# Values loaded head by head, two weight loads moved up the queue and wider filler matmuls in a fused attention and feed-forward kernel

## The chip, the core and the metric

The kernel runs on one core of a Trainium2 chip. The time is device microseconds from launch to end. Three runs of the kernel before gave 101.67, 102.06 and 102.32 us; the median is 102.06 us. One further execution was profiled: it took 102.56 us, of which 100.8 us are its span, from the first to the last instruction. The remaining 1.76 us lie around the span.

Engine names follow the profile: PE is the matrix engine (PEld its weight loads), DVE, ACT and POOL are the vector, scalar and general engines, SP issues nearly all DMAs from one queue. Each engine works through its own instructions in program order.

## What is computed

Linear attention with a polynomial sketch, and behind it a gated feed-forward layer. Batch 4, heads 4, sequence 1088, head width 32, sketch width 8; model width 128, inner width 1536.

```python
def phi(x):
    a = np.einsum('rd,bhsd->bhsr', S1, x)
    b = np.einsum('rd,bhsd->bhsr', S2, x)
    return np.einsum('bhsi,bhsj->bhsij', a, b).reshape(*x.shape[:-1], r * r)
q_p, k_p = phi(q), phi(k)
kv  = np.einsum('bhsf,bhsd->bhfd', k_p, v)
z   = np.sum(k_p, axis=2)
num = np.einsum('bhsf,bhfd->bhsd', q_p, kv)
den = np.einsum('bhsf,bhf->bhs', q_p, z)[..., None] + 1e-06
attn = num / den                              # then heads side by side: x, 4352 x 128
out = (np.maximum(x @ w_gate, 0) * (x @ w_val)) @ w_out
```

## The kernel before

**Layout.** Partition `32*h + p` of `k_sb[b]` and `q_sb[b]` holds 34 consecutive tokens of head `h`. The values lie otherwise: partition `32*a + p` of `v32[b]` holds nine tokens (seven for `a` = 3) of each of the four heads, 1152 bytes a head, since there the tokens are the rows of a matmul. `load_v(eng, b, a)` (L212) fills 32 partitions with all heads; four calls, in the order 0, 2, 1, 3, fill one batch.

**Loads.** SP issues, in this order: keys and queries of batch 0, its four value loads (L236), then `load_w(0)`, `load_w(1)` (gate and value weights, a third at a time, 256 KB each: wg0, wv0, wg1, wv1), `load_wo(0)`, keys of batch 1, `load_w(2)` (wg2, wv2), two more thirds of the output weights, queries of batch 1 (L263 to L270). The weights land in the buffers that later hold keys, queries and values of other batches, and are then cast to 16 bits by ACT (L425) or POOL (L427); `CAST` (L418) says by which.

**The plan.** All other work is a list of operations, each with an engine, an assumed duration, its predecessors and a due time. `Plan.run` (L89) places them once, when the program is built: it picks the next operation by earliest start and due time, gives out PSUM banks, and the program is then recorded in the order of the planned starts (L1091 to L1100). So the constants of the plan (`LAND`, the assumed landing times; `T0`, `U`, the due times of the feed-forward units; `act`, `pool` and others, assumed durations) fix the order on every engine, but not when anything really runs. On the chip an operation waits for its semaphores, and what stands behind it on its engine waits with it.

**Names used below.** `vc b h`: ACT casts two heads of the values of batch b to 16 bits (`K.vc`, L598). `kv b`: PE multiplies key features with these values (L601); `kve` evacuates them. `qsk`, `qt2`, `bw`, `dn`, `rd`, `an`, `qphi`: sketch, transpose, denominator and features of a group of query tokens. `qtr` with `qpt` (PE and ACT), or `qtd` (a DMA transpose issued by SP, L867): the features transposed. `num`, `x`: attention output of the group, the input of the feed-forward layer. The layer is cut into 103 units: `g u` and `v u` on PE (L950, L962), `relu u` on ACT (L955), the product `h u` on DVE (L972), or, in every sixth unit, a copy on ACT (L967) and the product on POOL (L977), and `o u` on PE (L984). Groups of units end with a copy `oe` and a store `st`. Units 0 to 5, 6 to 11 and 12 to 23 belong to the token groups of batch 0, unit 24 is the first of batch 1.

**Fillers.** `warm(n)` (L326) records matmuls of zeros over `n` columns, 128 at a time, wherever the plan leaves PE idle ahead of the first unit.

Two of the five feature products of batch 0's keys are on DVE (`own`, L488). The change leaves that as it is.

Of the kernel before, what the change touches and what calls it, by code (L numbers as in the profile page):

```python
# [146 lines left out]
def kernel(  # L147
# [12 lines left out]
    nc = tc.nc  # L160
# [7 lines left out]
    NC = S // 32  # L168
# [40 lines left out]
    def load_k(eng, b):  # L209
        eng.dma_start(out=k_sb[b][:, 0:NC * D], in_=flat(k, b))  # L210

    def load_v(eng, b, a):  # L212
        w = KX * D
        n = w if a < 3 or b < B - 1 else (KX - 2) * D
        src = v[b, 0]
        eng.dma_start(
            out=v32[b][32 * a:32 * a + 32, :, 0:n],
            in_=bass.AP(src.tensor, src.offset + a * w, [[NC * D, 32], [S * D, H], [1, n]]))

    def wcols(w, lo, hi):  # L220
        return w[:, lo * 128:hi * 128]
# [11 lines left out]
    nc.sync.dma_start(out=k_sb[0][:, KH:NC * D], in_=flat(k, 0)[:, KH:])  # L233
    nc.sync.dma_start(out=q_sb[0][:, 0:QA], in_=flat(q, 0)[:, 0:QA])
    nc.sync.dma_start(out=q_sb[0][:, QA:], in_=flat(q, 0)[:, QA:])
    for a in (0, 2, 1, 3):  # L236
        load_v(nc.sync, 0, a)
    bz = [sb([128, 2, 128], FP16, f"bz{b}") for b in range(B)]
    zero = sb([128, 128], FP16, "zero")
    nc.vector.memset(zero, 0.0)  # L240
# [22 lines left out]
    load_w(0)  # L263
    load_w(1)
    load_wo(0)
    load_k(nc.sync, 1)
    load_w(2)
    load_wo(1)
    load_wo(2)
    nc.sync.dma_start(out=q_sb[1], in_=flat(q, 1))  # L270
# [2 lines left out]
        eng.dma_start(out=q_sb[b], in_=flat(q, b))  # L273

    def load_vs(b):
        for a in (0, 2, 1, 3):
            load_v(nc.sync, b, a)


    id16 = sb([2 * R, 2 * R], FP32, "id16")  # L280
# [25 lines left out]
    nc.vector.memset(bz[0], 0.0)  # L306
    for i in range(2):
        nc.vector.memset(kT[i][:, NC * 32:], 0.0)
    nc.vector.memset(v32[B - 1][96:128, :, (KX - 2) * D:], 0.0)
# [16 lines left out]
    def warm(n):  # L326

        while n >= 32:
            m = min(n // 32 * 32, 128)
            nc.tensor.matmul(PS[:, W_BANK, 0:m], zero, zero[:, 0:m], start=True, stop=True)  # L330
            n -= m

    warm(3584)
    S_BANK = 6
# [46 lines left out]
    P.banks[W_BANK] = 13.0  # L381
    P.banks[S_BANK] = 6.0
    l_sx = Lease()
    T0, U, SLACK = 11.0, 0.68, 0.25
    D1 = 0.2

    TURN = ["ACT"] * 3 + ["DMA"] * 7
# [8 lines left out]
        return cols / 960.0 + 0.085  # L396

    def act(cols):
        return cols / 1200.0 + 0.045

    def pool(cols):
        return cols * 0.00188 + 0.07

    LAND = {"k0a": 3.6, "S": 4.3, "k0b": 4.25, "q0a": 5.6, "q0b": 7.35, "v0": 9.95,
            "wg0": 10.35, "wv0": 11.0, "wg1": 11.65, "wv1": 12.3, "wo0": 12.95, "k1": 15.6,
            "wg2": 16.25, "wv2": 16.9, "wo1": 17.5, "wo2": 18.1, "q1": 19.5}
    land = {n: P.landed(n, t) for n, t in LAND.items()}
    P.free["DMA"] = LAND["q1"]

    def bank(l, i=0):  # L410
# [4 lines left out]
    sa_op = P.add("DVE", "SA", 0.22, make_SA, [land["S"]], rec=0.07)  # L415
    wb_op = P.add("DVE", "WB", 0.15, make_WB, [land["S"]], rec=0.07)

    CAST = {"wg0": "ACT", "wv0": "POOL", "wg1": "ACT", "wv1": "POOL", "wo0": "POOL",  # L418
            "wg2": "ACT", "wv2": "ACT", "wo1": "ACT", "wo2": "POOL"}
    wcast = {}  # L420

    def cast(w, i, eng):
# [9 lines left out]
                         rec={"ACT": 0.13, "DVE": 0.07, "POOL": 0.0}[e])  # L432


    def load(name, fn, after):
        n = 4 if name[0] == "v" else 1
        i = P.add("SP", f"{name} issue", 0.44 * n, fn, after, rec=1.95 - 0.44 * n)
        land[name] = P.add("DMA", name, 2.7 if n == 4 else 1.4, None, [i], rec=0.15)
# [5 lines left out]
    load("k3", lambda: load_k(nc.sync, 3), [wcast["wg0"], wcast["wv0"], land["q2"]])  # L444
    load("q3", lambda: load_q(nc.sync, 3), [wcast["wg1"], wcast["wv1"], land["q2"]])
    load("v3", lambda: load_vs(3), [land["v2"]])

    class K:


        def __init__(self, b, prev):
# [39 lines left out]
            for n, (lo, hi) in enumerate(cut):  # L491
# [11 lines left out]
                else:  # L503
                    phis.append(P.add("POOL", f"kphi {b} {lo}", pool(cols),
                                      lambda lo=lo, hi=hi: self.phi(nc.gpsimd, lo, hi), dep))
            vc = [P.add("ACT", f"vc {b} {h}", 0.58, lambda h=h: self.vc(h), [land[f"v{b}"]],
                        rec=0.13) for h in range(2)]
            lm = Lease()
            self.lm = lm
            self.kvs = []  # L510
# [120 lines left out]
    class Q:  # L631
# [3 lines left out]
        def __init__(self, b, x0, n, i, ks, qt1, old):  # L635
            self.b, self.x0, self.n, self.ks = b, x0, n, ks
            i = i % NS
            self.abc, self.an = q_abc[i], q_an[i]
            self.dn, self.rd, self.bw = q_dn[i], q_rd[i], bw[i]
            first = b == 0 and x0 == 0  # L640
            self.first = first
            name = f"{b},{x0}"
            cols = n * 32
            wcs = [kk.wc_op for kk in ks]
            if first:
                la, lc = Lease(), Lease()
# [13 lines left out]
                e, eng = "DVE", nc.vector  # L660

            else:
                self.l4 = [Lease(2), Lease(2)]
                s1 = P.add("PE", f"qsk {name}", cols / 600.0 + 0.28 + 0.37 * (n > NX),
                           self.sk, qt1 + wcs + [wq_op], take=self.l4)
# [25 lines left out]
            self.t2_op = t2  # L691
            self.last = []
# [106 lines left out]
    class G:  # L799


        def __init__(self, qs, b, ks, x0, n, i, col, old, how):
# [6 lines left out]
            if qs.first:  # L809
                for x in range(n):  # L810
                    phis.append(P.add("DVE", f"qphi {name} {x}", 0.31,
                                      lambda x=x: self.phi(nc.vector, x, x + 1), [qs.o4],
                                      drop=[qs.la], rec=0.07))
                qs.la.left -= n
            else:
                phis.append(P.add("POOL", f"qphi {name}", pool(n * 256),
                                  lambda: self.phi(nc.gpsimd, 0, n), [qs.o4] + old))
            if how == "DMA":
                pt = P.add("SP", f"qtd {name}", 1.28, self.xpose, phis + old, rec=0.7)
                pt = P.add("DMA", f"qtd {name}", 0.6, None, [pt], rec=0.5)  # L820
            else:
                lt = Lease()
# [84 lines left out]
    class F:  # L907


        def __init__(self, u, grp, qg, js, prev, old):  # L910
# [14 lines left out]
            vv = P.add("PE", f"v {u}", cost, self.v, [qg.x_op, wcast[f"wv{third}"]], take=[lv], due=t + 0.2)  # L925
            if self.pool:
                a2 = P.add("ACT", f"vcp {u}", act(cols), self.vcp, [vv], drop=[lv], rec=0.13,
                           due=t + 0.6)
                h = P.add("POOL", f"hp {u}", 1.18, self.hp, [a, a2, old], due=t + 1.3)
# [113 lines left out]
    for n, (b, x0, w, parts) in enumerate(sets):  # L1043
# [6 lines left out]
        for gb, y, m in parts:  # L1050
# [80 lines left out]
```

## Time and profile before

| what | value |
|---|---|
| median of three runs | 102.06 us |
| profiled execution | 102.56 us, span 100.8 us |
| PE busy | 95.1 us, 94% of the span |
| DVE, ACT, POOL busy | 83.8, 82.2, 59.9 us |
| feed-forward matmuls g, v, o on the chain that ended last | 18%, 17%, 19% of the span |
| fillers on that chain | 7% |
| granted PE clock | full in all 40 slices |
| DMA | 13.28 MB, mean 132 GB/s; the first 20 us carry over 270 GB/s in most slices |

The profile counts an engine as busy while one of its instructions runs, fillers included. The chain of waits goes back from the last instruction: at each step to what released it, or to the instruction before it on its engine.

### The profile page before, as it was taken

What the parts mean: (1) busy time and instruction counts of PE and PEld (TensorE: products, weight loads), DVE (VectorE), ACT (ScalarE), POOL (GpSimd) and SP (SyncE); (2) the same over time, 40 slices, a digit from 0 to 9 for tenths busy, and PEclk for the clock granted to TensorE, in tenths of its full rate; (3) what the DMA queues carried; (4) which work ended last, traced back from release to release, by engine and by line L of the source; (5) the groups of instructions that cost most, each with busy time, mean ns of one, the idle gap of its engine ahead of it and who ended that gap; (6) DMA issues with size and microseconds to landing.
All of it is one profiled execution on the core that took longest, in us unless ns stands there. A gap on an engine that the chain in (4) does not pass through costs nothing.

```text
span 100.8 us, 3139 instructions
## 1 busy us (share of the span) xinstructions
PE 95.1 (94%) x1191; PEld 66.4 (66%) x1191; DVE 83.8 (83%) x181; ACT 82.2 (82%) x162; POOL 59.9 (59%) x64
## 2 busy tenths in 40 slices
PE   6999997999999899999999999999999999999960
PEld 6959895678775466656756676667666666667940
DVE  5989959899999989999998679978768587795960
ACT  3411968997999978999977769899899999989940
POOL 7157269399999399349973993489960314033100
PEclk9999999999999999999999999999999999999999
DMA  2999999499943696300426003001481300120031
GB/s 44 321 272 294 408 403 417 166 309 272 386 131 108 145 136 163 104 7 0 104 52 156 7 0 104 7 7 37 121 182 37 81 24 0 52 59 0 4 100 52
DMA packets 16783, 13.28 MB, mean 132 GB/s; under 512 B 8064, under 2 KB 14464, under 8 KB 16768
## 3 DMA queue, kind: packets, MB, share of 16 engines
q1 hardware_dynamic: 16736, 13.08, 45.8%
q8 instruction: 9, 0.15, 0.6%
q14 instruction: 6, 0.05, 0.1%
q10 hardware_dynamic: 32, 0.00, 0.0%
HBM read 9.14 MB, written 2.23 MB: 113 GB/s over the span
## 4 chain that ended last, share of the span: by engine, by line
PE 78%; POOL 7%; ACT 5%; DMA 3%; issue 2%; DVE 2%; ACTq 0%
PE ps L984 19%; PE ps L950 18%; PE ps L962 17%; PE ps L330 7%; POOL qqp L859 4%; PE ps L893 3%; ACT g_sb L955 3%; PE ps L728 3%; DMA qpt<-qqp 3%; PE ps L536 2%; PE ps L606 2%; POOL kp L593 1%; PE ps L564 1%; PE ps L877 1%; DVE qabc L734 1%
## 5 line engine op out<-in xcount | busy, mean ns | idle before, releaser
L972 DVE TENSOR_TENSOR ht<-g_sb,ps 128x512 f16<-128x512 f16 (+1 forms) x87 | 55.4, 672 | 10.1 <-ACT g_sb L955 5.5
L955 ACT ACTIVATE g_sb<-ps 128x512 f16<-128x512 f32 (+1 forms) x103 | 57.1, 610 | 4.9 <-PE ps L950 4.1
L950 PE MATMUL ps<-xT,wg 128*128 128x512 f16 (+1 forms) x120 | 38.3, 348 | 0.4 <-ACT wg L425 0.4
L984 PEld LDWEIGHTS <-ht 128*128 128x128 f16 x408 | 28.8, 98 | 14.0 <-POOL ht L977 2.5
L984 PE MATMUL ps<-wo,ht 128*128 128x128 f16 x408 | 36.5, 219 | 0.2
L962 PE MATMUL ps<-xT,wv 128*128 128x512 f16 (+1 forms) x120 | 36.5, 348 | 0.0
L977 POOL TENSOR_TENSOR ht<-g_sb,v_sb 128x512 f16<-128x512 f16 x16 | 18.7, 1170 | 19.3 <-ACT v_sb L967 13.2
L593 POOL TENSOR_TENSOR kp<-kab 128x512 f16<-128x512 f32 (+1 forms) x15 | 17.1, 1162 | 5.0 <-DVE kab L549 5.0
L962 PEld LDWEIGHTS <-wv 128*128 128x128 f16 x120 | 13.0, 115 | 5.1 <-issue 1.1
L859 POOL TENSOR_TENSOR qqp<-qan,qabc 128x1024 f16<-128x1024 f32 (+1 forms) x9 | 15.7, 1763 | 0.1
L950 PEld LDWEIGHTS <-wg 128*128 128x128 f16 x120 | 13.1, 114 | 3.7 <-issue 0.9
L967 ACT COPY v_sb<-ps 128x512 f32<-128x512 f32 x16 | 9.7, 605 | 0.0
L330 PE MATMUL ps<-zero 128*128 128x128 f16 (+2 forms) x85 | 7.7, 257 | 1.0 <-DVE maskkv L295 1.0
L330 PEld LDWEIGHTS <-zero 128*128 128x128 f16 x85 | 6.7, 119 | 1.4 <-DVE maskkv L295 1.0
L992 ACT ACTIVATE o_sb<-ps 128x512 f32<-128x512 f32 (+1 forms) x10 | 5.5, 546 | 1.9 <-PE ps L984 1.9
L599 ACT CAST v<-v 128x576 f16<-128x576 f32 x8 | 5.3, 700 | 1.5 <-DMA v<-in_v_dram 1.4
L734 DVE STREAM_TRANSPOSE qabc<-ps 128x512 f32<-128x512 f32 (+2 forms) x8 | 5.4, 695 | 0.7 <-PE ps L728 0.6
L1024 DVE STREAM_TRANSPOSE qT<-q_sb 128x576 f32<-128x576 f32 (+4 forms) x10 | 6.0, 611 | 0.0
L905 ACT CAST xT<-ps 128x512 f16<-128x512 f32 (+1 forms) x9 | 4.9, 550 | 1.1 <-PE ps L893 1.1
L893 PE MATMUL ps<-qpt,bz 128*128 128x512 f16 (+2 forms) x26 | 5.3, 305 | 0.4 <-DMA qpt<-qqp 0.4
L525 DVE STREAM_TRANSPOSE kT<-k_sb 128x544 f32<-128x544 f32 (+2 forms) x8 | 5.6, 725 | 0.0
L606 PEld LDWEIGHTS <-kp 128*128 128x128 f16 (+1 forms) x72 | 3.6, 98 | 1.3 <-issue 0.2
(85 smaller groups left out, 63.9 us busy)
## 6 DMA issues: line engine op xcount, KB each, us to landing
v<-in_v_dram SPq DMA_DIRECT2D x15, 144.0 KB, 4.5
out_dram<-o_sb SPq DMA_DIRECT2D x28, 64.0 KB, 1.7
k_sb<-in_k_dram SPq DMA_DIRECT2D x3, 544.0 KB, 5.4
q_sb<-in_q_dram SPq DMA_DIRECT2D x3, 544.0 KB, 7.1
k_sb<-in_moe_w_out_dram SPq DMA_DIRECT2D x2, 256.0 KB, 5.9
q_sb<-in_q_dram SPq DMA_DIRECT2D x1, 416.0 KB, 5.2
k_sb<-in_k_dram SPq DMA_DIRECT2D x1, 288.0 KB, 2.9
k_sb<-in_k_dram SPq DMA_DIRECT2D x1, 256.0 KB, 3.0
```

What stands on the lines that cost most here:

```text
L330: nc.tensor.matmul(PS[:, W_BANK, 0:m], zero, zero[:, 0:m], start=True, stop=True)
L593: eng.tensor_tensor(out=self.kp[:, lo:hi].rearrange("p x g (i a c) -> p (x g i) a c", i=2, a=R), in0=src[:, 0, :, :, None].to_broadcast([1 ...
L734: nc.vector.transpose(self.abc[:, 0:self.n, 2 * i:2 * i + 2].rearrange("p x h f -> p h x f"), PS[:, b0:b1 + 1, 0:self.n * 32].rearrange("p ...
L859: eng.tensor_tensor(out=self.qp[:, lo:hi].rearrange("p x g (i a c) -> p (x g i) a c", i=2, a=R), in0=a_in[:, :, :, None].to_broadcast([128 ...
L893: nc.tensor.matmul(o[:, 0:n * 128].rearrange("f (x t) -> f x t", x=n)[:, :, t], self.ks[b or 0].bz[:, p], self.pt[:, 0:n, p, t], start=(p ...
L950: nc.tensor.matmul(bank(self.lg)[:, y * W:(y + 1) * W], wblock(wg, j), x, start=True, stop=True, skip_group_check=True)
L955: nc.scalar.activation(out=self.gs[:, 0:self.cols], in_=bank(self.lg)[:, 0:self.cols], func=ACTF.Relu)
L962: nc.tensor.matmul(bank(self.lv)[:, y * W:(y + 1) * W], wblock(wv, j), x, start=True, stop=True, skip_group_check=True)
L967: nc.scalar.copy(out=self.vs, in_=bank(self.lv))
L972: nc.vector.tensor_tensor(out=self.ht[:, 0:w], in0=self.gs[:, 0:w], in1=bank(self.lv)[:, 0:w], op=ALU.mult)
L977: nc.gpsimd.tensor_tensor(out=self.ht, in0=self.gs, in1=self.vs, op=ALU.mult)
L984: nc.tensor.matmul(o[:, s], self.ht[:, y * W + s * 128:y * W + (s + 1) * 128], wo[:, j // 4, (j % 4) * DM:(j % 4 + 1) * DM], start=(j == 0 ...
```

## The change

Values: one DMA now takes one head and all 128 partitions, in the same place in SBUF as before. Its source is walked as 4 blocks of 32 rows of 288 numbers, its destination as 128 rows. In the built program the source pattern of such a load counts 4, 32, 288 and the destination pattern 128, 1, 288, while before both sides counted 32, 4, 288. There are again four loads for a batch; the last head of batch 3 takes two.

Queue: wg2 and wv2 are issued ahead of batch 1's keys. Casts: wv0 and wv1 go from POOL to ACT, wv2 from ACT to POOL. Fillers: one matmul covers up to 512 columns, by reading the same 128 columns up to four times. The plan's constants change, and batch 3's loads (k3, q3, v3) are issued only behind the DMA transposes of batch 1 (`gs[4].turn` is the second of the two).

```diff
-    def load_v(eng, b, a):
+    def load_v(eng, b, h):
         w = KX * D
-        n = w if a < 3 or b < B - 1 else (KX - 2) * D
-        src = v[b, 0]
-        eng.dma_start(
-            out=v32[b][32 * a:32 * a + 32, :, 0:n],
-            in_=bass.AP(src.tensor, src.offset + a * w, [[NC * D, 32], [S * D, H], [1, n]]))
+        src = v[b, h]
+
+        for lo, hi, n in [(0, 4, w)] if (b, h) != (B - 1, H - 1) else [(0, 3, w), (3, 4, w - 2 * D)]:
+            eng.dma_start(
+                out=v32[b][32 * lo:32 * hi, h, 0:n],
+                in_=bass.AP(src.tensor, src.offset + lo * w, [[w, hi - lo], [NC * D, 32], [1, n]]))
...
-    for a in (0, 2, 1, 3):
-        load_v(nc.sync, 0, a)
+    for h in range(H):
+        load_v(nc.sync, 0, h)
...
     load_wo(0)
+    load_w(2)
     load_k(nc.sync, 1)
-    load_w(2)
     load_wo(1)
...
-            m = min(n // 32 * 32, 128)
-            nc.tensor.matmul(PS[:, W_BANK, 0:m], zero, zero[:, 0:m], start=True, stop=True)
-            n -= m
+            m, w = (min(n // 128, 4), 128) if n >= 128 else (1, n // 32 * 32)
+            nc.tensor.matmul(PS[:, W_BANK, 0:m * w], zero,
+                             zero[:, None, 0:w].to_broadcast([128, m, w]), start=True, stop=True)
+            n -= m * w
...
-    T0, U, SLACK = 11.0, 0.68, 0.25
+    T0, U, SLACK = 11.0, 0.65, 0.25
+    E0 = 1.0
...
-    LAND = {"k0a": 3.6, "S": 4.3, "k0b": 4.25, "q0a": 5.6, "q0b": 7.35, "v0": 9.95,
-            "wg0": 10.35, "wv0": 11.0, "wg1": 11.65, "wv1": 12.3, "wo0": 12.95, "k1": 15.6,
-            "wg2": 16.25, "wv2": 16.9, "wo1": 17.5, "wo2": 18.1, "q1": 19.5}
+    LAND = {"k0a": 3.6, "S": 4.3, "k0b": 4.25, "q0a": 5.2, "q0b": 6.9, "v0a": 7.7, "v0b": 8.45,
+            "wg0": 9.3, "wv0": 9.94, "wg1": 10.58, "wv1": 11.22, "wo0": 11.86, "wg2": 12.5,
+            "wv2": 13.14, "k1": 15.5, "wo1": 16.14, "wo2": 16.78, "q1": 18.14}
...
-    CAST = {"wg0": "ACT", "wv0": "POOL", "wg1": "ACT", "wv1": "POOL", "wo0": "POOL",
-            "wg2": "ACT", "wv2": "ACT", "wo1": "ACT", "wo2": "POOL"}
+    CAST = {"wg0": "ACT", "wv0": "ACT", "wg1": "ACT", "wv1": "ACT", "wo0": "POOL",
+            "wg2": "ACT", "wv2": "POOL", "wo1": "ACT", "wo2": "POOL"}
...
-            vc = [P.add("ACT", f"vc {b} {h}", 0.58, lambda h=h: self.vc(h), [land[f"v{b}"]],
-                        rec=0.13) for h in range(2)]
+            vc = [P.add("ACT", f"vc {b} {h}", 0.58, lambda h=h: self.vc(h),
+                        [land[f"v{b}" if b else f"v0{'ab'[h]}"]], rec=0.13) for h in range(2)]
...
-            t = T0 + u * U + (D1 if u >= 6 else 0.0)
+            t = T0 + u * U + (D1 if u >= 6 else -E0)
...
+    for n in ("k3", "q3", "v3"):
+        issue[n].after.append(gs[4].turn)
+        gs[4].turn.succ.append(issue[n])
...
-                warm(int((o.start - at) * (1200 if o.start < WARM else 2280)))
+                warm(int((o.start - at) * 1200) if o.start < WARM else
+                     int((o.start - at - 0.1) * 2280))
```

What this does to the order of the instructions: on ACT the casts now stand `vc 0 0`, `qt2 0,0`, `vc 0 1`, wg0, wv0, `rdx`, wg1, `qpt 0,0`, `rdTe`, wv1, wg2, `relu 0`; before, wg0 and wg1 stood behind `qpt` and `rdTe`, and wg2 and wv2 behind `relu 3`. On PE all of `kv 0` stands ahead of `qsk 0,2`, and its first part ahead of `qc` and `w 0`; before, all three stood ahead of `kv 0`. `vc 1 0` stands ahead of `relu 9`, before behind `relu 13`. On SP the loads q2, k2, v1, v2 are followed by two stores and the two transposes of batch 1, and then by k3, q3, v3; before, k3 and q3 stood ahead of the first store and of v2.

More of the change, by code (lines that the diff above doesn't have):

```diff
@@ L275, in load_vs @@
     def load_vs(b):
-        for a in (0, 2, 1, 3):
-            load_v(nc.sync, b, a)
+        for h in range(H):
+            load_v(nc.sync, b, h)
     id16 = sb([2 * R, 2 * R], FP32, "id16")
@@ L308 @@
         nc.vector.memset(kT[i][:, NC * 32:], 0.0)
-    nc.vector.memset(v32[B - 1][96:128, :, (KX - 2) * D:], 0.0)
+    nc.vector.memset(v32[B - 1][96:128, H - 1, (KX - 2) * D:], 0.0)
     sel = sb([2 * R, 16, R], FP32, "sel")
@@ L398, in act @@
     def act(cols):
-        return cols / 1200.0 + 0.045
+        return cols / 1200.0 + 0.062
     def pool(cols):
         return cols * 0.00188 + 0.07
-    LAND = {"k0a": 3.6, "S": 4.3, "k0b": 4.25, "q0a": 5.6, "q0b": 7.35, "v0": 9.95,
-            "wg0": 10.35, "wv0": 11.0, "wg1": 11.65, "wv1": 12.3, "wo0": 12.95, "k1": 15.6,
-            "wg2": 16.25, "wv2": 16.9, "wo1": 17.5, "wo2": 18.1, "q1": 19.5}
+    LAND = {"k0a": 3.6, "S": 4.3, "k0b": 4.25, "q0a": 5.2, "q0b": 6.9, "v0a": 7.7, "v0b": 8.45,
+            "wg0": 9.3, "wv0": 9.94, "wg1": 10.58, "wv1": 11.22, "wo0": 11.86, "wg2": 12.5,
+            "wv2": 13.14, "k1": 15.5, "wo1": 16.14, "wo2": 16.78, "q1": 18.14}
     land = {n: P.landed(n, t) for n, t in LAND.items()}
@@ L432 @@
                          rec={"ACT": 0.13, "DVE": 0.07, "POOL": 0.0}[e])
+    issue = {}
     def load(name, fn, after):
         n = 4 if name[0] == "v" else 1
-        i = P.add("SP", f"{name} issue", 0.44 * n, fn, after, rec=1.95 - 0.44 * n)
-        land[name] = P.add("DMA", name, 2.7 if n == 4 else 1.4, None, [i], rec=0.15)
+        issue[name] = i = P.add("SP", f"{name} issue", (0.62 if n == 4 else 0.44) * n, fn, after,
+                                rec=(1.95 - 0.62 * n if n == 4 else 1.5))
+        land[name] = P.add("DMA", name, 1.5 if n == 4 else 1.4, None, [i], rec=0.15)
     load("v1", lambda: load_vs(1), [wcast["wo2"]])
@@ L443 @@
     load("v2", lambda: load_vs(2), [wcast["wg2"], wcast["wv2"], land["v1"]])
-    load("k3", lambda: load_k(nc.sync, 3), [wcast["wg0"], wcast["wv0"], land["q2"]])
-    load("q3", lambda: load_q(nc.sync, 3), [wcast["wg1"], wcast["wv1"], land["q2"]])
+    load("k3", lambda: load_k(nc.sync, 3), [wcast["wg0"], wcast["wv0"]])
+    load("q3", lambda: load_q(nc.sync, 3), [wcast["wg1"], wcast["wv1"]])
     load("v3", lambda: load_vs(3), [land["v2"]])
@@ L663, in __init__ @@
                 self.l4 = [Lease(2), Lease(2)]
-                s1 = P.add("PE", f"qsk {name}", cols / 600.0 + 0.28 + 0.37 * (n > NX),
+                s1 = P.add("PE", f"qsk {name}", cols / 600.0 + 0.34 + 0.37 * (n > NX),
                            self.sk, qt1 + wcs + [wq_op], take=self.l4)
@@ L815, in __init__ @@
             else:
-                phis.append(P.add("POOL", f"qphi {name}", pool(n * 256),
+                phis.append(P.add("POOL", f"qphi {name}", pool(n * 256) - 0.02 * n,
                                   lambda: self.phi(nc.gpsimd, 0, n), [qs.o4] + old))
@@ L819, in __init__ @@
                 pt = P.add("SP", f"qtd {name}", 1.28, self.xpose, phis + old, rec=0.7)
+                self.turn = pt
                 pt = P.add("DMA", f"qtd {name}", 0.6, None, [pt], rec=0.5)
@@ L924, in __init__ @@
                       due=t + 0.35)
-            vv = P.add("PE", f"v {u}", cost, self.v, [qg.x_op, wcast[f"wv{third}"]], take=[lv], due=t + 0.2)
+            vv = P.add("PE", f"v {u}", cost, self.v, [qg.x_op, wcast[f"wv{third}"]], take=[lv], rec=0.07,
+                       due=t + 0.2)
             if self.pool:
@@ L928, in __init__ @@
                            due=t + 0.6)
-                h = P.add("POOL", f"hp {u}", 1.18, self.hp, [a, a2, old], due=t + 1.3)
+                h = P.add("POOL", f"hp {u}", 1.13, self.hp, [a, a2, old], rec=0.06,
+                          due=t + 1.3)
             else:
```

## The prediction, written before the changed kernel ran

> **What bounds the kernel now.** I first read the busy time of each engine by stages of the span (stretch, length, busy time and instructions of PE, PEld, DVE, ACT, POOL, granted PE clock, DMA share, GB/s).
>
> ```profile
> 0.00:14.00 14.00, 12.99 (x220) 11.23 (x221) 11.87 (x58) 5.92 (x13) 6.78 (x19) 1.00 0.89 281
> 14.00:19.00 5.00, 4.07 (x50) 2.77 (x48) 3.74 (x7) 4.39 (x9) 4.22 (x5) 1.00 0.91 359
> 19.00:30.00 11.00, 10.97 (x159) 8.57 (x158) 10.56 (x20) 10.24 (x22) 9.96 (x9) 1.00 0.85 263
> 30.00:37.00 7.00, 6.60 (x89) 3.97 (x88) 6.54 (x13) 6.71 (x14) 5.32 (x5) 1.00 0.71 107
> 37.00:60.00 23.00, 23.00 (x318) 14.70 (x318) 20.54 (x38) 20.12 (x38) 17.58 (x16) 1.00 0.31 75
> ```
>
> From 37 us on PE has no idle time left, up to 95 us (35.00 of 35.00 us in the next stretch). So what PE loses or gains before 37 us reaches the end in full, and nothing in the change makes PE's later work shorter. Before 37 us three places give: the first unit starts at 13.76 us, PE idles 0.93 us from 14 to 19 us and 0.40 us from 30 to 37 us. I then read the start in order of time.
>
> ```profile
> 2.63 1.86 SPq L216 DMA_DIRECT2D v<-in_v_dram  x4
> 9.99 1.25 ACT L599 CAST v<-v 128x576 f16<-128x576 f32 x2 [1.37 <-DMA v<-in_v_dram]
> 11.15 0.40 ACT L777 COPY rdx<-qrd 128x256 f32<-128x256 f32 x1
> 12.56 1.35 PE L330 MATMUL ps<-zero 128*128 128x128 f16 x22
> 13.00 0.36 DVE L900 TENSOR_TENSOR xT<-ps,rdT 128x256 f16<-128x256 f32 x1
> 13.76 0.39 PE L950 MATMUL ps<-xT,wg 128*128 128x256 f16 x2
> ```
>
> ACT waits 1.37 us for the values, and `rdx`, whose input `rd` is ready at 10.27, starts at 11.15 behind the two casts. The input of unit 0 is done at 13.36, but 22 fillers hold PE until 13.9. How fast the loads come is in the DMA's totals for two stretches, 5.5 to 9 us (values) and 9.5 to 17 us (weights and keys), and in the page's row on ACT's queue, which carries S1 and S2 alone:
>
> ```profile
> DMA packets 691, 0.86 MB, mean 246 GB/s; under 512 B 77, under 2 KB 552, under 8 KB 691
> DMA packets 1344, 3.07 MB, mean 410 GB/s; under 512 B 145, under 2 KB 145, under 8 KB 1341
> q10 hardware_dynamic: 32, 0.00, 0.0%
> ```
>
> With 32 partitions a load the values come at 246 GB/s, with 128 partitions the rest comes at 410. And S1 and S2 have 8 rows each, 16 rows together; the other 16 of the 32 packets I read as completions, 8 a load. A load whose outer pattern counts 8 thus ran on 8 engines, not on 16.
>
> **The values' loads, the main term.** The new source pattern counts 4 on the outside, the destination 128. No load in the trace has unequal sides. Nearest are S1 and S2, the only ones with an outer count under 16, and there the count was the number of engines. From the other side stand loads of 128 partitions like the keys: 16 engines, 410 GB/s. I take the first: four engines at 410/16 = 25.6 GB/s each, 102 GB/s. Four loads of 147 KB are 0.59 MB and take 5.8 us, 1.44 us a head. They start when batch 0's keys and queries are through on those engines: 1.11 MB, of which 0.89 MB moved between 2 and 5 us; the rest at the 330 GB/s of then takes 0.7, so 5.7 us. From the return of the rate to over 340 GB/s (about 9.1 us) to the end of ACT's wait are 0.8 us; I take 0.7 to landing. The heads then land at 7.8, 9.3, 10.7 and 12.2 us; today ACT has all at 9.99.
>
> [...]
>
> What queues behind. On those four engines every later load waits: 256 KB are 0.64 us a load at 410 GB/s, so wg0 lands at 12.8 (11.5 + 0.64 + 0.7), wv0 13.5, wg1 14.1, wv1 14.7, wo0 15.4, wg2 16.0, wv2 16.7, and batch 1's keys (1.36 us) at 18.0, 2.7 us later than their 15.3. ACT's order now has `vc 0 1` ahead of everything up to `relu 0`. Back-to-back casts start 0.52 us apart in the trace (17.16, 17.67, 18.19). So: `vc 0 1` 12.2; wg0 12.8; wv0 13.5; `rdx` 14.0; wg1 14.3; `qpt` 14.8; `rdTe` 15.3; wv1 15.6; wg2 16.1; `relu 0` 16.6, against 14.19 today: **+2.4**. PE's order has both halves of `kv 0` ahead of `qsk 0,2`, so PE also stands until 12.8, and `num`, `x` and `g 0` fit in at about 16: the fillers ahead of them cost nothing here.
>
> Back comes what is idle from 14 to 19 us today, 0.93 us, as PE waits there for casts of wg2 and wv2 (17.16 to 18.30) and for `qtr` behind POOL; wg2 is now cast ahead of `relu 0`: **-0.9**, between 0 and -0.9, the upper value since 12 us of matmuls are then ready.
>
> Batch 1's values meet the same four engines: q1, q2 and k2 go ahead (0.56 MB each, 1.36 us; 18.0 for k1, two weights, then three such: 23.4), then 2.9 us for two heads, so 26.3 + 0.7 = 27.0. `vc 1 0` moves ahead of `relu 9`, which starts at 24.6 today and would at about 26.1. ACT, with all `relu` behind it, waits 0.9 us, and again for the second pair at 29.9. In SP's queue the two stores and `qtd` then wait for v1 and v2, whose semaphores they reuse; today `qtd` goes at 32.33, 2.2 us after its input, as v2's last load waited for q3 to land (29.95). I put the gain of moving k3 and q3 behind against that wait. Together **+1.0**, between 0 and +2.5.
>
> **The rest.** Casts: ACT takes two of 0.52 from POOL and gives one; counted above. Fillers: 3584 columns at the start take 3.17 us as 28 pieces and, by columns, as 7; ahead of `g 0` 1568 columns instead of 22 x 128 = 2816. A piece of 512 can hold PE 0.22 us longer. Zero where the end is set by ACT, -0.3 (13.36 to 13.76) in the first rival. Issue: a value load holds SP 0.43 to 0.46 us today (1.86 for four); unequal sides may need more, at most the 0.59 of the first S load, so 0 to 0.6 for four, hidden by the 5 us to landing. k3, q3 and v3, issued behind `qtd`, so from about 36 us, land at the page's 5.4 us for keys near 41.8; today the first transpose of k3 is at 40.08 and the first cast of v3 at 40.49, the second ones at 46.51 and 44.08. I take nothing, as the second ones wait in any case, and up to 1.7 us is in the +2.5; so is v3's four-engine time, should the transposes of batch 2 stand behind it.
>
> Sum: 2.4 - 0.9 + 1.0 = +2.5 us; 102.56 + 2.5 = 105.1 for a run like the profiled one, and as that stands 0.5 us over the median of 102.06, **104.6 us**. Its own range: +1.1 to +4.4, 103.2 to 106.5.
>
> **First rival: sixteen engines, faster.** The loads spread, 0.59 MB takes 1.44 us, all values land at 5.7 + 1.4 + 0.7 = 7.8 instead of 9.9. For it: the destination now spans 128 partitions, and every load of that kind reads at 410 GB/s. Against: row S1/S2. Then `rdx` starts at 10.3 instead of 11.15, but `qpt` still waits for `qphi` (10.89), so `num` gains 0.4 and the shorter filler 0.3; from 14 to 19 us up to 0.9, from 30 to 37 us up to 0.4, since `qtd` no longer stands behind q3. That is 2.0 at most. ACT is busy 4.39 of 5 us in that stretch, so I take 0.4 + 0.3 + half of 0.9 = 1.15: 100.9 us, between 100.0 and 101.5. It decides if the four loads of batch 0 land within 1.5 us of each other.
>
> [...]
>
> **Second rival: no change.** The values land early, but the start is held elsewhere: the key features on POOL end at 9.54 us (three products of L593 from 6.41), `kv 0` cannot end before, and `qsk 0,2`, today at 9.91, now stands behind it. That costs up to 0.7 on the way to `qphi 0,2` (14.62) and takes back the 0.7 at the start; the weights' 0.4 remains or not: 101.6 to 102.5, 102.0 us. For it: POOL is at 84% from 14 to 19 us and 91% from 19 to 30.
>
> **How the numbers follow.** Four engines 0.58, all of it slower; sixteen and faster 0.27; sixteen and no change 0.15. One per cent is 1.0 us, about what can be told from no change here. Faster 0.27, same 0.15, slower 0.58. The range holds the forecast's own up to 106.5 (about 0.52), the whole second rival, and reaches down to 100.6 for about half of the first: 100.6 to 106.5.
>
> **What would show it.** Four-engine loads: the four landings of batch 0's values 1.4 us apart, the DMA's rate near 100 GB/s about 9 to 11 us, `relu 0` near 16.6, ACT waiting for values at `vc 0 1` and at `vc 1 0`. Sixteen: landings 0.4 us apart, a rate near 400 right through, `rdx` near 10.3. The queue step is wrong if wg0 lands before the last head. The forecast also fails if PE's clock is granted less after PE has stood for 2 us with no fillers: no row shows that, it would add to the end.

## The result, and the profile after

The changed kernel took 112.61, 113.42 and 114.55 us, median 113.42 against 102.06; the ratio is 1.108, 95% interval 1.095 to 1.121. Slower, as forecast, but by 11.4 us and not by 2.5: outside the range of 100.6 to 106.5. The profiled execution is the one of 114.55 us, with a span of 112.8. Medians take all executions; ratios and intervals leave out slow and disturbed ones, among them the profiled one here (mean granted clock 0.920, the other two 0.939 and 0.954) and one each of `e6_fillers` (238.69 us) and `e13_sixteen` (319.4 us, the profiled one, so that its trace is read for the number of packets alone).

The same stages of the span as before (stretch, length, busy time and instructions of PE, PEld, DVE, ACT, POOL, granted PE clock, DMA share, GB/s), and the page's row of the granted clock in 40 slices:

```profile
0.00:14.00 14.00, 9.52 (x92) 5.33 (x93) 9.30 (x49) 3.15 (x7) 5.55 (x17) 0.84 0.77 224
14.00:19.00 5.00, 4.00 (x54) 2.51 (x54) 1.91 (x5) 3.36 (x7) 1.22 (x2) 0.50 0.87 291
19.00:30.00 11.00, 11.00 (x156) 8.10 (x155) 9.91 (x20) 9.55 (x19) 7.94 (x8) 0.97 0.50 180
30.00:37.00 7.00, 5.59 (x60) 3.98 (x58) 5.21 (x11) 5.82 (x12) 4.77 (x5) 1.00 0.34 114
37.00:60.00 23.00, 20.44 (x211) 11.82 (x209) 17.29 (x32) 16.46 (x32) 14.80 (x13) 0.85 0.43 128
```

```profile
PEclk9996555999999997559999999999999999999998
```

PE loses time in all three places that were not full before, and after 37 us too. The clock, full in all slices before, is halved from 9.5 to 19.7 us, from 43.6 to 50.5, and in the last 0.9 us. Then the start in order of time (start, length, engine, line, operation, idle time before it and what ended that):

```profile
2.63 2.60 SPq L217 DMA_DIRECT2D v<-in_v_dram  x4
9.95 0.67 ACT L605 CAST v<-v 128x576 f16<-128x576 f32 x1 [2.53 <-DMA v<-in_v_dram]
14.27 0.67 ACT L605 CAST v<-v 128x576 f16<-128x576 f32 x1 [3.49 <-DMA v<-in_v_dram]
15.89 0.40 ACT L783 COPY rdx<-qrd 128x256 f32<-128x256 f32 x1
19.37 1.01 PE L331 MATMUL ps<-zero 128*128 128x512 f16 x4
20.23 0.39 PE L959 MATMUL ps<-xT,wg 128*128 128x256 f16 x2
20.66 1.08 ACT L964 ACTIVATE g_sb<-ps 128x512 f16<-128x512 f32 x2 [0.48 <-PE ps L959]
```

`relu 0` in the kernel before:

```profile
14.19 1.09 ACT L955 ACTIVATE g_sb<-ps 128x512 f16<-128x512 f32 x2 [0.85 <-PE ps L950]
```

The second pair of heads comes 4.3 us behind the first and holds ACT for 3.49 us; `relu 0` starts at 20.66 against 14.19. The third place is SP's queue ahead of unit 24; first the kernel before, then the changed one, and the queue's own waits for values at the stores (us in total, times, longest):

```profile
25.61 4.66 SPq L216 DMA_DIRECT2D v<-in_v_dram  x4
30.37 1.79 SPq L1001 DMA_DIRECT2D out_dram<-o_sb  x4
32.33 2.68 SPq L867 DMA_TRANSPOSE qpt<-qqp  x2
```

```profile
24.77 8.11 SPq L217 DMA_DIRECT2D v<-in_v_dram  x8
32.98 8.21 SPq L1010 DMA_DIRECT2D out_dram<-o_sb  x8
41.36 2.69 SPq L874 DMA_TRANSPOSE qpt<-qqp  x2
```

```profile
SPq L1010 <- DMA v<-in_v_dram: 3.7, 3, 1.8
```

Eight value loads (v1, v2), then the eight parts of two stores, which reuse the semaphores of those loads, so that the last three go out only as the last three heads land, and behind them the two transposes of batch 1: 41.36 against 32.33. Counted at the starts of `relu`, in the two profiled executions:

| stretch | before, us | after, us | more |
|---|---|---|---|
| to unit 0 | 14.19 | 20.66 | +6.47 |
| unit 0 to 8 | 9.49 | 7.23 | -2.26 |
| unit 8 to 24 | 13.65 | 20.98 | +7.33 |
| unit 24 to the end | 65.23 | 65.68 | +0.45 |
| profiled execution | 102.56 | 114.55 | +11.99 |

That the loads ran on four engines is read from the page's row on SP's queue (packets, MB, share of 16 engines), before and after:

```profile
q1 hardware_dynamic: 16736, 13.08, 45.8%
q1 hardware_dynamic: 16559, 13.10, 39.1%
```

If every load leaves one completion on each engine it uses (the author's reading, which the counts here fit), before's 16 value loads leave 16 x 16 = 256; the new ones 15 x 4, and 3 + 16 for the last head's two, together 79. The difference, 177, is 16736 - 16559, and in the DMA records all of it are packets of 4 bytes (1376 before, 1199 after).

### The profile page after: what moved, and what is told of

Read it like the earlier page. It is cut to its first block, busy times and chain, and to the rows that moved or that the text cites. A ratio compares the mean times of both kernels' runs of the same rounds, so it can differ in the third digit from the quotient of the medians.

```text
span 112.8 us, 3028 instructions
## 1 busy us (share of the span) xinstructions
PE 99.9 (89%) x1125; PEld 64.7 (57%) x1125; DVE 84.8 (75%) x181; ACT 83.4 (74%) x163; POOL 59.4 (53%) x63
## 3 DMA queue, kind: packets, MB, share of 16 engines
q1 hardware_dynamic: 16559, 13.10, 39.1%
## 4 chain that ended last, share of the span: by engine, by line
PE 78%; DMA 11%; SPq 3%; ACT 2%; DVE 2%; issue 1%; DVEq 0%; ACTq 0%
PE ps L993 21%; PE ps L971 21%; PE ps L959 20%; DMA v<-in_v_dram 9%; PE ps L900 4%; PE ps L734 3%; DMA qpt<-qqp 3%; PE ps L612 2%; PE ps L542 2%; PE ps L331 2%; SPq L217 2%; PE ps L884 1%; DVE ht L981 1%; PE ps L570 1%; PE ps L788 1%
## 5 line engine op out<-in xcount | busy, mean ns | idle before, releaser
L959 PE MATMUL ps<-xT,wg 128*128 128x512 f16 (+1 forms) x120 | 39.9, 356 | 1.3 <-ACT g_sb L964 1.3
L971 PE MATMUL ps<-xT,wv 128*128 128x512 f16 (+1 forms) x120 | 39.8, 355 | 1.0 <-ACT g_sb L964 0.9
L993 PEld LDWEIGHTS <-ht 128*128 128x128 f16 x408 | 29.4, 99 | 18.0 <-DVE ht L981 3.4
L993 PE MATMUL ps<-wo,ht 128*128 128x128 f16 x408 | 38.3, 222 | 0.3 <-DVE ht L981 0.2
L959 PEld LDWEIGHTS <-wg 128*128 128x128 f16 x120 | 13.5, 115 | 4.2 <-issue 2.4
L612 PE MATMUL ps<-v,kp 128*128 128x64 f16 (+1 forms) x72 | 5.0, 204 | 4.5 <-ACT v L605 4.5
L331 PE MATMUL ps<-zero 128*128 128x512 f16 (+5 forms) x19 | 7.2, 504 | 1.0 <-DVE maskkv L296 1.0
L900 PE MATMUL ps<-qpt,bz 128*128 128x512 f16 (+2 forms) x26 | 6.0, 336 | 1.7 <-DMA qpt<-qqp 1.7
```

The costliest lines, as they stand in the source:

```text
L331: nc.tensor.matmul(PS[:, W_BANK, 0:m * w], zero, zero[:, None, 0:w].to_broadcast([128, m, w]), start=True, stop=True)
L612: nc.tensor.matmul(m[:, 64 * p:64 * p + 64], self.kp[rows, x, p], v16[self.b][rows, 2 * p:2 * p + 2, x * D:(x + 1) * D], start=(x == 0 and ...
L900: nc.tensor.matmul(o[:, 0:n * 128].rearrange("f (x t) -> f x t", x=n)[:, :, t], self.ks[b or 0].bz[:, p], self.pt[:, 0:n, p, t], start=(p ...
L959: nc.tensor.matmul(bank(self.lg)[:, y * W:(y + 1) * W], wblock(wg, j), x, start=True, stop=True, skip_group_check=True)
L971: nc.tensor.matmul(bank(self.lv)[:, y * W:(y + 1) * W], wblock(wv, j), x, start=True, stop=True, skip_group_check=True)
L993: nc.tensor.matmul(o[:, s], self.ht[:, y * W + s * 128:y * W + (s + 1) * 128], wo[:, j // 4, (j % 4) * DM:(j % 4 + 1) * DM], start=(j == 0 ...
```

## The experiments

Each was run beside the kernel before on the same chip. Theory at the start: the four-engine loads set the time; rival: the order that the plan's new constants make.

### Quarter loads in the changed kernel, whole and in part

`e1_quarters`: the changed kernel with all value loads as before, four quarters of 32 partitions a batch (`load_q4` is the old `load_v`; `load_vs` likewise).

```diff
-    for h in range(H):
-        load_v(nc.sync, 0, h)
+    for a in (0, 2, 1, 3):
+        load_q4(nc.sync, 0, a)
```

> The changed kernel with all values loaded by 32 partitions and four heads as before; everything else as changed. Four-engine theory: the whole loss goes, values land near 9.9 us, the first relu near 15, 100.5 to 103 us. Order theory (the new order on PE and ACT and the store order on SP cost the time, whatever the loads do): still above 108 us.

`e2_heads_v0` makes this edit in `load_vs` alone, so that batch 0 stays by head; `e3_heads_later` makes it for batch 0 alone.

> The changed kernel with only batch 0's values loaded by head, the others by quarters. Four-engine theory: the first relu stays near 20.7 us (+6.5), batch 1's transposes go out as soon as their features are there, so 107 to 109 us. If the late transposes are a mere echo of the late start, the loss stays whole: 112 to 114 us.

> The changed kernel with batch 0's values by quarters and the others by head. Four-engine theory: the first relu near 15 us, but the stores and transposes behind the value loads on SP are late, PE idles near 35 us and its clock drops: 105 to 108 us. If everything comes from the start: 101 to 103 us.

`e4_before_heads` is the kernel before with the change's `load_v` and nothing else of it.

```diff
-    for a in (0, 2, 1, 3):
-        load_v(nc.sync, 0, a)
+    for h in range(H):
+        load_v(nc.sync, 0, h)
```

> The kernel before with nothing changed but the value loads, by head. Four-engine theory: the values of batch 0 land at 10 and 14.2 us as in the changed kernel, the weights behind them, so 108 to 113 us although no order is changed. Order theory: 102 to 104 us.

| kernel | median us | ratio, 95% | relu 0 | relu 24 |
|---|---|---|---|---|
| e1 | 107.78 | 1.053 (1.048 to 1.059) | 17.99 | 41.87 |
| e2 | 110.56 | 1.071 (1.065 to 1.077) | 21.45 | 46.63 |
| e3 | 109.02 | 1.063 (1.057 to 1.068) | 17.93 | 44.17 |
| e4 | 115.94 | none; before 102.43 | 19.95 | 49.23 |

(`relu` starts are those of the profiled execution.) The loads by head cost 13.5 us alone by the medians (e4; its four executions lie between 114.84 and 117.73), and taking them out of the change gives back only 5.6 (113.42 - 107.78): neither theory has it all. None of the four times lies in a range that was set for it: e1 is just below 108, e2 between its two ranges, e3 1.0 and e4 2.9 us above. Batch 0's heads cost 2.8 us by the medians (e2 against e1; 1.8% by the ratios), the later ones 1.2 (e3 against e1), both together 5.6, more than the two added. In e3 SP's queue shows the later ones by themselves: start 17.93, yet the transposes of batch 1 go at 38.70 (e1: 36.42). What was left to explain is that e1 itself is 5.35 us slower than the kernel before beside it (102.43).

### What is wrong with the order

`e5_landings`: e1, with the plan's landing times set to where quarter loads land.

```diff
-            "q0a": 5.2, "q0b": 6.9, "v0a": 7.7, "v0b": 8.45,
-            "wg0": 9.3, "wv0": 9.94, "wg1": 10.58, "wv1": 11.22, "wo0": 11.86, "wg2": 12.5,
+            "q0a": 5.2, "q0b": 7.3, "v0a": 9.7, "v0b": 9.7,
+            "wg0": 10.3, "wv0": 10.9, "wg1": 11.6, "wv1": 12.2, "wo0": 12.6, "wg2": 13.2,
...
```

> e1_quarters with landing times in the plan that fit its loads (values at 9.7 instead of 7.7 and 8.45, weights and queries to match), so that the plan puts qc, w and qsk of batch 0 ahead of kv again. Order theory (a plan made for values at 7.7 puts PE and ACT behind values that land at 9.7): the first relu near 14.5 us, the clock stays whole, 100.5 to 103 us. If the other edits (fillers, queue, casts) cost the time: still 105 us or more.

104.45 us, ratio 1.021 (1.014 to 1.029), between the two ranges. `relu 0` starts at 14.03 and PE's clock stays full: e1's loss at the start was an order that had put `kv 0` ahead of work that was ready, for values planned at 7.7 and 8.45. The new landing times also moved v2 behind the first store again on SP, as before the change; what that is worth was not tried by itself. But unit 24 came at 39.07, 1.74 us later than before, though unit 8 came 0.5 sooner.

`e6_fillers`: e1 with 3800 columns of fillers ahead of `kv 0`, where PE had stood.

```diff
     for o in todo:
         if o.eng == "PE":
+            if o.name == "kv 0 0 0":
+                warm(3800)
```

> e1_quarters with 3800 columns of zero matmuls ahead of kv 0, where PE stands for the values; order unchanged. Clock theory (the halved clock from 10.3 to 17.1 us costs some 2 us of the start): the clock stays whole, the first relu near 16.5 instead of 18, 105 to 106.5 us. If the order alone costs: 107 to 108.5 us.

106.56 us (the median of 105.27, 106.04, 107.09 and 238.69), ratio 1.036 (1.028 to 1.044); `relu 0` at 15.96 instead of 17.99. PE in two stages of e1 (columns as above):

```profile
6.00:9.50 3.50, 2.73 (x43) 1.69 (x28) 3.25 (x10) 0.38 (x1) 3.03 (x3) 1.00 1.04 280
9.50:14.00 4.50, 3.55 (x60) 2.82 (x59) 1.88 (x8) 3.37 (x7) 0.86 (x3) 0.59 1.06 414
```

and in e6:

```profile
6.00:9.50 3.50, 3.48 (x47) 1.99 (x32) 3.33 (x11) 0.38 (x1) 2.86 (x3) 1.00 1.04 239
9.50:14.00 4.50, 3.81 (x74) 2.65 (x72) 2.22 (x9) 3.53 (x8) 0.88 (x2) 1.00 1.06 404
```

Zeros in the gap kept the clock at 1.00 in e6, where it was 0.59 in e1. The halved clock was worth 2.0 us of the start in e1; the other 1.9 (15.96 to 14.03) went only with the order.

`e9_vc_later` is e5 with 4.2 us instead of 1.5 assumed from a value load's issue to its landing, so that `vc 1 0` stands behind `relu 13` as before. `e10_no_hook` is e5 without the lines that put k3, q3 and v3 behind the transposes.

```diff
-P.add("DMA", name, 1.5 if n == 4 else 1.4, None, [i], rec=0.15)
+P.add("DMA", name, 4.2 if n == 4 else 1.4, None, [i], rec=0.15)
```

```diff
-    for n in ("k3", "q3", "v3"):
-        issue[n].after.append(gs[4].turn)
-        gs[4].turn.succ.append(issue[n])
```

> As e5_landings, but the plan assumes 4.2 us instead of 1.5 from a value load's issue to its landing, so that vc 1 0 stands behind relu 13 again, as before. In e5 ACT waited 1.45 us for vc 1 0 and unit 24 came 1.7 us later than in the kernel before, though unit 8 came 0.5 us sooner. If that wait is the cause, the wait is gone, relu 24 starts near 37.6 and the time is 102.6 to 103.4. If the order on SP (k3, q3, v3 behind the transposes) is the cause, it stays at 104.2 to 104.7.

> As e5_landings, but k3, q3 and v3 no longer wait in the plan for the transposes of batch 1. If the order on SP is what e5 lost, relu 24 starts near 37.6 and the time is 102.6 to 103.4; if ACT's wait at vc 1 0 is, it stays at 104.2 to 104.8, with relu 24 near 39.

e9: 102.40 us, ratio 0.998 (0.994 to 1.002), `relu 24` at 37.43. e10: 106.94, ratio 1.034 (1.026 to 1.041), `relu 24` at 41.60, above both ranges: putting k3, q3 and v3 behind the transposes is no loss here, and without it the wait grows. The first cast of batch 1's values in e5, e9 and e10:

```profile
25.95 0.67 ACT L604 CAST v<-v 128x576 f16<-128x576 f32 x1 [1.45 <-issue]
```

```profile
27.62 1.25 ACT L604 CAST v<-v 128x576 f16<-128x576 f32 x2
```

```profile
27.09 0.67 ACT L604 CAST v<-v 128x576 f16<-128x576 f32 x1 [2.63 <-DMA v<-in_v_dram]
```

In e9 it finds its values there. In e5 and e10 it stands ahead of `relu 9`, and what stands behind it on ACT waits with it. From `relu 8` to `relu 9` pass 0.95 us in the kernel before, 3.38 in e5, 1.86 in e9, 4.55 in e10, 3.87 in the changed kernel. So by the medians e1's loss is 3.3 us for the landing times (107.78 to 104.45) and 2.05 for the place of batch 1's cast (104.45 to 102.40); e9 can't be told from the kernel before.

### The order fitted to four engines

`e11_heads_landings`: the changed kernel, loads by head, with the plan's landings taken from its own trace (later heads 7 us for four).

```diff
-            "q0a": 5.2, "q0b": 6.9, "v0a": 7.7, "v0b": 8.45,
-            "wg0": 9.3, "wv0": 9.94, "wg1": 10.58, "wv1": 11.22, "wo0": 11.86, "wg2": 12.5,
+            "q0a": 5.2, "q0b": 6.9, "v0a": 9.9, "v0b": 14.2,
+            "wg0": 14.5, "wv0": 15.1, "wg1": 15.7, "wv1": 16.35, "wo0": 17.0, "wg2": 17.7,
...
-P.add("DMA", name, 1.5 if n == 4 else 1.4, None, [i], rec=0.15)
+P.add("DMA", name, 7.0 if n == 4 else 1.4, None, [i], rec=0.15)
```

> The changed kernel with its loads by head, but with the plan's landing times set to those of its own trace (values of batch 0 at 9.9 and 14.2, weights from 14.5 on, batch 1's keys at 19.7, four heads of a later batch 7 us). If the four-engine loads alone set the time, the order cannot help: relu 0 near 20.5 and 112.5 to 114. If a good half of the loss is an order made for landings that do not come, as with the quarter loads (107.78 to 104.45), relu 0 comes near 18.5 and the time is 108 to 110.

108.22 us, ratio 1.051 (1.044 to 1.058); `relu 0` at 17.37, clock full. Against e9, whose plan fits its quarter loads in the same way, four engines cost 5.8 us (108.22 - 102.40) when the order allows for them; 5.2 of the 11 (113.42 - 108.22) come from an order made for landings that do not come.

### The number of engines alone

`e13_sixteen`: the changed kernel and its order, with the source of each value load walked as 32 blocks of 4.

```diff
-in_=bass.AP(src.tensor, src.offset + lo * w, [[w, hi - lo], [NC * D, 32], [1, n]]))
+in_=bass.AP(src.tensor, src.offset + lo * w, [[NC * D, 32], [w, hi - lo], [1, n]]))
```

> The changed kernel, its plan and order untouched, with the source of each value load walked as 32 blocks of 4 instead of 4 of 32 (the last head of batch 3 as 32 of 3 and its rest): the same bytes go to the same partitions, but the tokens of a head stand in other rows, so the output is another one. Outer count 32, so 16 engines by the count of packets. If the number of engines is what the loads by head cost, all values of batch 0 land near 8 us, relu 0 starts near 13.5 and the time is 100 to 102. If the sum lies in the order of the plan or in the layout by head, it stays above 107, as with quarter loads in this plan (107.78).

102.12 us, ratio 0.9995 (0.996 to 1.003), 0.1 above the first range. Packets: 16752, 16 more than before, as one load more on 16 engines makes it. Bytes, destinations and the order of instructions are those of the changed kernel. The rows of the source are read in another order, but a packet of a value load takes 51 ns by the median in the changed kernel and with these loads (`e15_sixteen_later`) alike. So in this order of instructions the whole 11 us hang on the number of engines: by the packets 4 with an outer count of 4 (16559) and 16 with one of 32 (16752).

`e14_before_sixteen` puts the same loads into the kernel before.

> The kernel before with the loads of e13_sixteen alone (tokens in other rows, so another output). With four-engine loads in this place the time was 115.94. If the engines are the cause, values land 1 to 1.5 us before the quarter loads' 9.9 and the time is 101.0 to 102.3; if loads by head cost something else, above 104.

101.55, 105.07, 105.96 and 106.05 us: one in the first range and three in the second, so that what the loads are worth in this order stays open. Values are cast from 8.36 us without a wait (before 9.99) and `relu 0` starts at 13.98. In the profiled run (105.07) the loss is later:

```profile
36.37 1.03 PE L894 MATMUL ps<-qpt,bz 128*128 128x512 f16 x2 [2.34 <-DMA qpt<-qqp]
```

PE stood 2.34 us for a transpose (0.40 in the kernel before), and its clock was halved from 36.1 to 39.5. Why the transpose was late stays open.

`e15_sixteen_later`: e13 with e9's 4.2 us, to see where the earlier values go.

> As e13_sixteen (sixteen engines, tokens in other rows, another output), with the plan's 4.2 us instead of 1.5 from a value load's issue to its landing, so that vc 1 0 stands behind relu 12 and not ahead of it. If the early cast still costs with 16 engines, as it cost 2 us with quarter loads, the time falls from e13's 102.1 to 100.5 to 101.5; if it costs only where the values come late, it stays within 0.5 of 102.1. At the start the values are cast from about 8.4 on and relu 0 starts near 13.3 if nothing else holds it (the first rival's 0.9 before 14.19), near 14 if the key features do (the second rival).

102.90 us, ratio 0.999 (0.995 to 1.004), where e13 has 0.9995 (on another chip, so that the medians differ by 0.8): with 16 engines the place of `vc 1 0` decides nothing. ACT at the start:

```profile
7.46 0.67 ACT L605 CAST v<-v 128x576 f16<-128x576 f32 x1 [0.58 <-DMA v<-in_v_dram]
8.56 0.67 ACT L605 CAST v<-v 128x576 f16<-128x576 f32 x1 [0.27 <-DMA v<-in_v_dram]
...
10.90 0.40 ACT L783 COPY rdx<-qrd 128x256 f32<-128x256 f32 x1
...
14.79 0.62 ACT L428 CAST wg<-v 128x512 f16<-128x512 f32 x1 [1.57 <-DMA v<-in_moe_w_gate_dram]
15.31 1.08 ACT L964 ACTIVATE g_sb<-ps 128x512 f16<-128x512 f32 x2
```

The two casts start 2.5 and 2.0 us sooner than before, `rdx` 0.25, the first `g 0` 0.32 (13.44). Then the cast of wg2, now ahead of `relu 0`, waits 1.57 us for its load, and `relu 0` starts 1.1 us later than before.

### The rest of the change

`e7_before_wide` is the kernel before with the 512-column fillers, `e8_before_queue` with wg2 and wv2 ahead of batch 1's keys, the new casts, and landings to match.

```diff
-            m = min(n // 32 * 32, 128)
-            nc.tensor.matmul(PS[:, W_BANK, 0:m], zero, zero[:, 0:m], start=True, stop=True)
-            n -= m
+            m, w = (min(n // 128, 4), 128) if n >= 128 else (1, n // 32 * 32)
+            nc.tensor.matmul(PS[:, W_BANK, 0:m * w], zero,
+                             zero[:, None, 0:w].to_broadcast([128, m, w]), start=True, stop=True)
+            n -= m * w
```

```diff
-    load_k(nc.sync, 1)
     load_w(2)
+    load_k(nc.sync, 1)
...
-    CAST = {"wg0": "ACT", "wv0": "POOL", "wg1": "ACT", "wv1": "POOL", "wo0": "POOL",
-            "wg2": "ACT", "wv2": "ACT", "wo1": "ACT", "wo2": "POOL"}
+    CAST = {"wg0": "ACT", "wv0": "ACT", "wg1": "ACT", "wv1": "ACT", "wo0": "POOL",
+            "wg2": "ACT", "wv2": "POOL", "wo1": "ACT", "wo2": "POOL"}
```

> The kernel before with fillers of up to 512 columns in place of 128, same columns in all, nothing else. If fillers only hold the clock: 101.5 to 103 us, same. If pieces of 512 columns hold PE when work comes or the clock rises later: 103 to 105 us.

> The kernel before with wg2 and wv2 issued ahead of batch 1's keys and the changed casts, landing times of these moved in the plan, nothing else. If the early weights take back PE's 0.9 us between 14 and 19: 100.8 to 102 us. If ACT's two more casts ahead of relu 0 cost as much: 102 to 103.5 us.

e7: 104.49 us, ratio 1.016 (1.006 to 1.026), `relu 0` at 14.32 and `relu 24` at 37.62 (before 14.19 and 37.33). Its profiled run (106.51 us) lost time at 74 to 80 us, where PE, having stood 2.0 us for a transpose, ran 3.4 us at half clock; there are no fillers there. Whether fillers have part in that, and in the 1.6%, is open. e8: 102.72, ratio 1.006 (1.002 to 1.010): unit 4 comes 1.4 us sooner, unit 24 0.3, the end does not.

`e12_two_queues` is the kernel before with two of batch 0's four quarter loads issued from ACT's queue.

```diff
-        load_v(nc.sync, 0, a)
+        load_v(nc.scalar if a > 1 else nc.sync, 0, a)
```

> The kernel before with one edit: of batch 0's four quarter loads, two (a = 2, 3) are issued from ACT's queue. If the 246 GB/s of the value loads come from one half of the partitions being served at a time, both halves now move together: ACT waits under 0.7 us for the values instead of 1.37, and the time is 101.2 to 101.9. If the packets of 1152 bytes or the 16 engines set the rate, the wait stays at 1.3 to 1.5 and the time at 102.0 to 102.6.

```profile
10.42 1.25 ACT L599 CAST v<-v 128x576 f16<-128x576 f32 x2 [1.76 <-DMA v<-in_v_dram]
```

103.13 us, ratio 1.005 (1.002 to 1.008): the values come 0.4 us later than in the kernel before, not sooner, and the wait of 1.76 us lies outside both ranges. What sets the 246 GB/s of the quarter loads stays open. No version found beats the kernel before.

## Why the prediction was right in kind and wrong in size

Of the terms of the sum, +2.4 became +6.5, -0.9 became -2.3 and +1.0 became +7.3. (The terms' own bounds add up to +1.5 to +4.9, not to the +1.1 to +4.4 that the prediction gives; 113.4 is outside either.)

**Four engines: right.** The packet counts show it (the 177 packets fit counts of 4 and of 3), and e13, 102.12 us with an outer count of 32, that they are the cause. The number itself was the author's estimate from row S1/S2, where 8 rows a load left 8 completions.

**1.44 us a head: somewhat small for loads by themselves, too small beside others.** DMA's totals in the changed kernel from 6 to 7 us (values almost alone), then from 10 to 12 us:

```profile
DMA packets 75, 0.09 MB, mean 88 GB/s; under 512 B 1, under 2 KB 72, under 8 KB 75
```

```profile
DMA packets 381, 0.61 MB, mean 307 GB/s; under 512 B 30, under 2 KB 148, under 8 KB 381
```

The packets between 512 bytes and 2 KB are the values' (1152 bytes): 71 in 1 us, then 118 in 2 us, 59 in 1 us, while the weights' 2048-byte packets pass. The 88 GB/s are 1.7 us a head, where the prediction had 102 GB/s. In the DMA records one value packet takes 51 ns by the median up to 9 us and some 73 from 10 us on; the second head takes 1.7 us, the third 2.0, the fourth 2.5. The prediction let every later load stand behind the heads; their packets ran beside them (307 GB/s, where it looked for a rate near 100). Only completions stand behind, 0.6 us apart: SP reissues on the semaphores of wg0, wv0, wg1, wv1 at 14.58, 15.19, 15.82, 16.44, against 12.8 to 14.7 predicted. `vc 0 1` at 14.27 instead of 12.2: +2.1.

**From there to `relu 0` 4.4 us were set; 6.39 passed.** ACT did not set it, PE did. The chain of waits (start, length, what):

```profile
15.00 0.64 PE ps L612 x9
15.63 0.72 PE ps L331 x3
16.35 0.87 PE ps L734 x32
...
18.73 0.43 PE ps L331
19.15 0.43 PE ps L900 x2
19.58 0.80 PE ps L331 x4
```

L331 are the fillers: 0.72 + 0.43 + 0.80 = 1.95 us on the path, at half clock, where the prediction said that they cost nothing. (Its count of the fillers that stood there before is high: the 22 pieces hold 2720 columns, the last being one of 32, not 2816.) A filler is recorded for a gap of the plan and runs whether the gap is there or not. The caveat at the end of the prediction, a lower clock after PE has stood for 2 us, came true: PE stood 2.12 and 2.35 us for the casts. It had no term in the sum. Without fillers in this place no kernel was tried.

**The 0.9 us coming back: too small.** 2.26 came back by unit 8, as the weights had landed and been cast by then. But such a gain did not last in the runs with quarter loads: e8 and e9 reach unit 8 0.9 and 0.8 us sooner and unit 24 within 0.3. "What PE loses or gains before 37 us reaches the end in full" is true only of what is still there at unit 24: from there to the end of the span it is 63.45 us before, 63.9 after and 62.6 to 64.6 in the experiments other than e7 and the disturbed trace of e13.

**ACT and SP in batch 1, +1.0 between 0 and +2.5: this step failed.** 7.33 us were lost between units 8 and 24. The prediction priced ACT's two waits at batch 1's heads and, for `qtd`, set the gain from k3 and q3 against the semaphores. It did not add up that *eight* heads, v1 and v2, stand ahead of the stores and transposes on the same four engines: in the DMA records their packets run from 26.62 to 40.38 us, 1.72 us a head. By its own numbers (23.4, eight times 1.44, 0.7 to landing) `qtd` would have gone at 35.6, 3.3 us late. It went 9.0 late: the eight heads began 3.2 us later than the prediction had it, as SP could issue k2 ahead of them only at 23.94, and took 2.2 us more. The chain shows it:

```profile
41.36 2.82 DMA qpt<-qqp
44.18 0.05 issue
44.23 1.04 PE ps L900 x2
```

and PE's half clock behind it (unit 24 starts inside it, at 48.87):

```profile
43.60:50.50 6.90, 6.27 (x42) 3.53 (x43) 2.69 (x6) 2.31 (x5) 3.79 (x4) 0.51 0.71 220
```

Quarter loads in the same order (e1) tell the two parts of the 7.33 apart. From `relu 8` to `relu 9`, where ACT stands for the values, the changed kernel loses 2.9 us on the kernel before, where the prediction set 0.9, and e1 loses 3.1: that part comes with the early place of `vc 1 0`, with quarter loads as well. From `relu 9` to `relu 24` it loses 4.4 (17.11 us against 12.70) and e1 nothing (12.56): that part is the heads ahead of the transposes, half clock included. `e11_heads_landings`, by head with another order, takes 17.14 there.

**Zeros.** Issue: four value loads hold SP 2.60 us instead of 1.86, 0.74 more where 0.6 was the bound, hidden as said. k3, q3, v3 behind `qtd`: no wait of a batch 3 cast in the changed kernel, and e10 is slower than e5 without the move, where `vc 1 0` stands early.

**The rivals.** First: it set the landing with 16 engines at 7.8 and the gain at 1.15. In e15 the casts at 7.46 and 8.56 bear out the landing, the first `g 0` 0.32 sooner is about half of the 0.7 set for the start, and in place of the half of 0.9 set for the weights ACT waits for wg2. Its 100.9 did not come, e13 gave 102.12. Second: it set 102.0 us, and that is what 16 engines give, but by luck, as its mechanism does not show: the key features on POOL end at 9.14 in e15 and `qsk 0,2` starts at 10.09, 0.18 late and not 0.7.

## What to carry to other kernels

Before a load is reshaped, write down the outermost count of both its patterns, and count the completions in the trace afterwards; one dimension moved outward cost 11% here, and with the larger one outside again (e13) all of it came back. Sum a slow transfer over everything that shares its queue's semaphores up to the first instruction that the critical engine needs, not up to its own reader. An order fixed by assumed landings multiplies an error in them: the same four-engine loads cost 5.8 us in an order that knew them and 11 in one that did not.

## What the runs showed of the hardware

**The clock fell with short stands.** Half clock came with PE stands of 2.12 us (changed kernel), 1.72 (e1) and 2.34 (e14), and held for 3.41 us (e14, from 36.1 to 39.5) or a multiple (10.24 and 6.83 in the changed kernel). In the 3.41 us ahead of the drop PE was busy for 2.45 and 1.47 us in the changed kernel, 1.84 in e1, 1.36 in e14. No threshold follows. With as little work the clock also stayed full, in stretches that lie whole steps of 3.41 us from a drop: 2.01 us busy from 29.98 to 33.39 in the changed kernel, 1.79 from 27.38 to 30.79 in e1, 1.73 from 33.47 to 36.88 in e4, with stands of 1.30, 1.52 and 1.68 us. Two stands close together, 0.87 and 1.69 us, came ahead of the second drop in the changed kernel; 0.84 and 1.69 in e3 did not bring one. In the kept traces (without e13's) every stand of 1.72 us or more came with half clock.

**A 16 KB packet of instructions took 0.96 to 1.34 us of a DMA engine**, nine times in the profiled run of the kernel before. In e5, between 23.6 and 24.8 us, all else was through, and the last packet of v1 started only at 24.71, just as such a packet of 1.05 us, begun at 23.67, ended:

```profile
DMA packets 3, 0.02 MB, mean 16 GB/s; under 512 B 0, under 2 KB 2, under 8 KB 2
...
q8 instruction: 1, 0.02, 5.5%
q1 hardware_dynamic: 2, 0.00, 1.1%
```

The last load of v1 had 15 of its 16 completions by 24.00 and the sixteenth at 25.81, and ACT's cast went at 25.95. So the late packet is what ACT's 1.45 us waited for, which the profile puts down to nothing; that the instruction packet held it up is likely, but was not tried by itself.
